# Attention with normalised q and k, planned by its own scheduler: first rows prepared separately, later second load, exact start times in the plan, last stores after the branch

## Chip, cores and metric

One core of one Trainium2 chip. The metric is the device time of one execution in microseconds (us). The kernel before ran three times: 594.15, 594.32 and 594.42 us, median 594.32 us. A measurement of this kernel can tell about 0.2% (1.2 us) from no change.

## The reference

There are 32 heads of 2048 rows and 20 columns, in bf16. For each head

```
qn = q / (sqrt(sum(q*q)) + 1e-6)          # each row by its own length
kn = k / (sqrt(sum(k*k)) + 1e-6)
logits = (qn @ kn.T) * t[head]
out = softmax(logits) @ v
```

Every head has 2048 x 2048 logits, 134 million in all, and each needs an exponential. The matrix products are thin (20 columns), so the exponentials are the bulk of the work.

## The kernel before

**Units of work.** Heads are taken in eight groups of four (`hg`), and the queries of a group in four blocks of 512 columns, so there are 32 blocks of four heads. A *unit* is one head's 128 keys against one block's 512 queries; a block has 64 units (4 heads x 16 key rows `r`), the kernel 2048. The four heads lie on four 32-partition strips, so their matmuls run beside each other on TensorE (PE).

**Two ways to the exponential.** Way A: two units are multiplied into psA (L793), and ScalarE (ACT) takes one `exp` over 128x1024 (L995, a *wave*). Way D: one unit is multiplied into a bank of psD (also L793), VectorE (DVE) turns it into int16 bits of an f16 by a scale and an offset (L361, called `P1`), GpSimd (POOL) makes two shifted copies by an integer addition (L374), and the sum of four products with v (L815, "PV") approximates the exponential. D units are taken four at a time (one key row of all four heads, a *quad*). At the end of a block DVE transposes the result (L386, the drain), divides (L400, L401), and a DMA stores it.

**Preparation.** Per group, q and k are squared and summed on DVE, their inverse lengths found, rows scaled into qpad and kpad, and these are transposed into qT and kT by DMA (L446) or, for the first key rows of group 0, by PE matmuls with an identity (L624, L658) and copies out of psum (L636, L639, L664). In group 0 rows 0 to 3 of q and k go first and together: `prep_ops(0, 0, 4, 0, 2)` gives one square, one sum, one root on ACT, then 1e-6, the reciprocal, k's scaling, t into q's factor, q's scaling. Rows 4 to 15 of k and then of q follow with priority 1.5.

**The order of the work** is made at build time: `make_plan` simulates the five engines in steps of `DT` = 0.005 us with costs per operation (`dve`: 0.069 us plus a rate; `ACT0`: 0.0633 us plus columns), picks for each engine the best ready operation by priority (P1 has 1, a lower number goes first), and writes down each engine's order. On the chip the engines follow those orders and wait on semaphores only. An operation of the plan begins at the step at which the loop sees it. `ORDER` is a string with one letter for each ten waves; a letter picks a set of rules from `CHOICES`. `D_FROM` = 0.12 is the share of a group's 256 units that must be issued before way D begins. `HEAT0` = 18 matmuls on zeros run on PE at the start, and `step_heat` puts 128-column ones into later PE gaps. A group's loads are asked for by `plan_group` on SyncE's (SP) queue, for group 1 as soon as `LOAD1` = 0 allows it.

**Branch on t.** There are two plans, one with way D and one without it. The first instructions are common; then each engine loads a flag (L1432) and branches (L1433). The last two stores, one on SP's queue and one on ACT's, are inside the branch; behind it only SP waits for them (L1439), and then all engines meet (L173).

Of the kernel before, what the change touches and what calls it, by code (L numbers as in the profile page):

```python
# [33 lines left out]
ORDER = "01i6e8h7238em08g57h5hi2i0gi1j2i0lgea8aa50a567i6538abh965h237050"  # L34

PARTS = ((0, 4), (4, 16))
NH = 4
# [7 lines left out]
D_FROM = 0.12  # L45
# [14 lines left out]
DT = 0.005  # L60
# [4 lines left out]
HEAT0 = 18  # L65
# [6 lines left out]
ACT0 = .0633  # L72
LOAD0 = 2.75
TRL = 2.25
TRK = 1.2
# [15 lines left out]
LOAD1 = 0  # L91
# [65 lines left out]
def bass_standalone__qk_norm__prompt_kernel(  # L157
# [15 lines left out]
    with ExitStack() as es:  # L173
# [45 lines left out]
        out_sems = {}  # L219

# [27 lines left out]
        def prep_ops(hg, r0, r1, a0=0, a1=2, pool=False):  # L248
# [106 lines left out]
            return ops  # L355

# [112 lines left out]
        def make_plan(share):  # L469
# [88 lines left out]
            for ap_, x, key in zs:  # L558
                want_dve(Op("DVE", "z", lambda e, ap_=ap_, x=x: e.memset(ap_, x), ["idn"] * (key[0] == "idb"), [key], 0.07, 0.3), 0)
            n0 = [("num", a) for a in range(8)]  # L560
            for b in (1, 2, 3):
                want_dve(Op("DVE", "z", lambda e, b=b: e.tensor_single_scalar(n4[:, :, b:b + 1], n4[:, :, 0:1], float(b), ALU.add),
                            n0, [("num", -b)], 0.08, 0.4), 0)
            nums = n0 + [("num", -b) for b in (1, 2, 3)]
            want_dve(Op("DVE", "z", lambda e: e.transpose(numT, num), nums, ["numT"], 0.15, 0.4), 0)
            want_dve(Op("DVE", "z", lambda e: e.tensor_tensor(numE, num, numT, ALU.is_equal), nums + ["numT"], ["numE"], 0.15, 0.4), 1.6)
            i4, e4 = idn[:, :].rearrange("p (a b) -> p a b", b=32), bass.AP(accT, numE.offset, [numE.ap[0], [0, 4], [1, 32]])
            want_dve(Op("DVE", "z", lambda e: e.tensor_tensor(i4, i4, e4, ALU.mult), ["idn", "numE"] + [("idb", a) for a in range(4)], ["idn", ("accT", 0)], 0.25, 0.4), 1.6)
# [6 lines left out]
            def t_load():  # L575
                src = bass.AP(t.tensor, 0, [[0, 128], [1, H]])
                want_sp(dma("ldt", lambda e: e.dma_start(tb16[:, :], src), [], ["tb"], 0.1, 3.2))
                want_dve(dve("flag", H, R1, lambda e: e.tensor_reduce(tmx[:, :], tb16[:, :], AXIS_X, ALU.max, apply_absolute_value=True), ["tb"], ["flag"]), 1.4)
                want_dve(Op("DVE", "z", lambda e: e.memset(tb2[:, :, :, :], 1.0), [], ["tb1"], 0.1, 0.2), 1.45)
                want_dve(dve("z", H, R1, lambda e: e.tensor_copy(tb2[:, :, 0, :], tb16[:, :].rearrange("p (g h) -> p g h", h=NH)), ["tb1", "tb"], ["tb2"]), 1.45)  # L580
# [13 lines left out]
            for o in prep_ops(0, 0, 4, 0, 2):  # L594
                if o.name == "nrm":
                    o.eng = "ACT"
                    act_ops.append(P.link(o))
                    a = Op("ACT", "tab", lambda e: e.activation(act_scr[:, 16:32], act_scr[:, 16:32], ACT.Exp),
                           ["scr"], ["scr1"], 1.5, 1.6)
# [22 lines left out]
            psQ = psD[:, QW:2 * QW]  # L622
            for w_, pad, T, bank, key in (("k", kpad, kT, psD, ("psD", 0)), ("q", qpad, qT, psO, ("psD", OB(0)))):
                mms = [lambda e, r=r, w_=w_, pad=pad, bank=bank: e.matmul((bank if w_ == "k" or r < 2 else psQ)[:, r * 128:(r + 1) * 128],  # L624
                                                                   pad[0][:, r, :, :].rearrange("p h d -> p (h d)"), idn[:, :])
                       for r in range(4)]
                op = Op("PE", "T" + w_, None, [(w_ + "pad", 0, r) for r in range(4)] + [(w_ + "z", 0), "idn"],
                        [key] + [("psD", 1)] * (w_ == "q"))
                op.info = mms
                pe_pre.append(P.link(op))  # L630

            kk, qq = [("kT", 0, r) for r in range(4)], [("qT", 0, r) for r in range(4)]
# [16 lines left out]
            pe_mid = []  # L649
            gate = ("qT", 0, 1)  # L650
            for r0, r1, a0, a1 in ((4, 16, 1, 2), (4, 16, 0, 1)):
                for o in prep_ops(0, r0, r1, a0, a1):
                    if o.name == "sq":
                        o.reads.append(gate)
                    want_dve(o, 1.5)
                if a0 == 1:

                    mms = [lambda e, r=r: e.matmul(psD[:, (r - 4) * 128:(r - 3) * 128],  # L658
                                                   kpad[0][:, r, :, :].rearrange("p h d -> p (h d)"), idn[:, :]) for r in range(4, 8)]
                    op = Op("PE", "Tk", None, [("kpad", 0, r) for r in range(4, 8)] + [("kz", 0), "idn"], [("psD", 0)])  # L660
                    op.info = mms
                    pe_mid.append(P.link(op))
# [4 lines left out]
                    gate = ("kT", 0, 7)  # L667
# [192 lines left out]
            def pv_round(c):  # L860
# [85 lines left out]
            def step_pe0():  # L946
                nonlocal a_sb, d_sb, issued_a, issued_d
                if pe_pre:
                    if all(d.done is not None and d.done + SEML <= now for d in pe_pre[0].deps):
                        pe_put(pe_pre.pop(0), "tp", range(NH))  # L950
                        return True
                    return False
                if pe_mid and all(d.done is not None and d.done + SEML <= now for d in pe_mid[0].deps):
                    pe_put(pe_mid.pop(0), "tp", range(NH))
# [179 lines left out]
            def step_act():  # L1134
# [7 lines left out]
                finish(a, now, a.cost, a.lat)  # L1142
                free_["ACT"] = now + a.cost
# [55 lines left out]
            def step_dve():  # L1199
# [6 lines left out]
                else:  # L1206
                    dve_todo.remove(best)
                    if o.name == "P1" and o.info[0] + 1 < DBANKS and (sum(x[2].name == "P1" for x in dve_todo) >= S.JOINB or next_wave() < JOINT) and sum(not kept(b_) for b_ in range(DBANKS)) >= S.JOINK:
                        nxt = next((x for x in dve_todo if x[2].name == "P1" and x[2].info == (o.info[0] + 1, o.info[1] + 1)), None)
                        if nxt is not None and ready_at(nxt[2]) is not None and ready_at(nxt[2]) <= now + S.JOIN:  # L1210
# [5 lines left out]
                            st = max(now, ready_at(o))  # L1216
# [4 lines left out]
                finish(o, now, o.cost, o.lat)  # L1221
                free_["DVE"] = now + o.cost
# [186 lines left out]
        def issue(eng, e, plan, i0, i1):  # L1409
            P, waits = plan  # L1410
            outs = [o for o in P.order["SP"] + P.order["ACT"] if o.name == "out"]
            for o in P.order[e][i0:i1]:
                if e == "SP" and o.name == "out" and o.sem is ends[0]:
                    for x in outs:
                        if x.sem not in ends:
                            eng.wait_ge(x.sem, 16)
# [7 lines left out]
                elif o.sem is not None:  # L1424
                    o.emit(eng).then_inc(o.sem, 16)
# [3 lines left out]
        def run(eng, e):  # L1429
# [5 lines left out]
            with eng.Else():  # L1435
                issue(eng, e, plans[1], cut[e], None)
            if e == "SP":
# [50 lines left out]
```

## Time and profile before

| what | value |
|---|---|
| median of 3 runs | 594.32 us |
| the profiled execution's own time | 594.49 us |
| its span, first to last instruction | 592.7 us |
| busy: PE, DVE, ACT, POOL | 581.3, 574.6, 580.4, 500.9 us |
| exp on ACT | 628 instructions, 576.2 us |
| P1 on DVE | 768 instructions, 488.1 us |
| first exp begins, last exp ends | 9.47 us, 585.96 us |

The profiled execution is 1.79 us longer than its span: that part lies around the recorded instructions. Times inside the trace are counted from the span's start. ACT and DVE are both busy through nearly the whole span, and the two ways share the units between them, so the time is read as three pieces: the head before the first exp, the stretch of exps, and the tail behind the last one.

### The profile page before, as it was taken

To read this page: it belongs to the slowest core of one execution; us is meant where nothing else is said; L and a number is where in the kernel's file an instruction comes from. 1 tells how busy PE (TensorE), PEld (TensorE's weight loads), DVE (VectorE), ACT (ScalarE), POOL (GpSimd) and SP (SyncE) were. 2 spreads that over 40 slices of the span, in tenths; PEclk is the share of its full clock that TensorE was granted. 3 is DMA by queue.
4 is the path that set the end of the run, shared out by engine and by line. 5 is a ranking of instruction groups with operands and counts; after the bars stand their busy time and mean duration, and the time that the engine had idled before them with its cause. 6 is when DMAs were issued, how large, how long until landed. Compare 5 with 4: busy or idle time off the path is not lost.

```text
span 592.7 us, 16383 instructions
## 1 busy us (share of the span) xinstructions
PE 581.3 (98%) x6768; PEld 160.2 (27%) x6768; DVE 574.6 (97%) x1016; ACT 580.4 (98%) x636; POOL 500.9 (84%) x951
## 2 busy tenths in 40 slices
PE   8999999999999999999999999999999999999996
PEld 4432222322223222232223222222222232222221
DVE  7999999999999999999999999999999999999993
ACT  6999999999999999999999999999999999999995
POOL 2488899878988799887998889987999978999994
PEclk9999999999999999999999999999999999999999
DMA  8700405205051131504033005330406104010000
GB/s 116 108 2 14 104 2 45 47 8 110 3 59 32 31 86 13 79 1 101 19 22 71 1 19 100 24 69 10 92 2 76 32 2 72 2 25 4 7 11 11
DMA packets 132145, 24.20 MB, mean 41 GB/s; under 512 B 121312, under 2 KB 132064, under 8 KB 132064
## 3 DMA queue, kind: packets, MB, share of 16 engines
q1 hardware_dynamic: 131264, 22.96, 24.6%
q8 instruction: 55, 0.90, 0.6%
q14 instruction: 26, 0.21, 0.1%
q10 hardware_dynamic: 800, 0.12, 0.1%
HBM read 7.87 MB, written 2.62 MB: 18 GB/s over the span
## 4 chain that ended last, share of the span: by engine, by line
ACT 87%; PE 10%; DVE 2%; POOL 1%; issue 0%
ACT pA L995 87%; PE psD L815 4%; PE psA L793 3%; PE psA L616 1%; PE psD L612 1%; POOL dS L374 1%; DVE dI L361 0%; PE psD L793 0%; PE psD L749 0%; DVE ssum L294 0%; DVE accT L386 0%; DVE sqs L291 0%; DVE kpad L338 0%; PE psD L616 0%; DVE ost L401 0%
## 5 line engine op out<-in xcount | busy, mean ns | idle before, releaser
L995 ACT ACTIVATE pA<-psA 128x1024 f16<-128x1024 f32 (+1 forms) x628 | 576.2, 1201 | 0.5 <-PE psD L793 0.2
L374 POOL INT64_ADD dS<-dI x935 | 494.5, 545 | 71.3 <-DVE ost L401 14.3
L361 DVE TENSOR_SCALAR dI<-psD 128x512 int16<-128x512 f32 (+1 forms) x768 | 488.1, 695 | 4.3 <-PE psD L793 2.5
L793 PE MATMUL psA<-qT,kT 32*128 32x512 bf16 x1256 | 246.4, 384 | 3.7 <-ACT pA L995 1.0
L793 PE MATMUL psD<-qT,kT 32*128 32x512 bf16 x795 | 237.6, 383 | 0.1
L815 PE MATMUL psD<-dS,vaug 128*22 128x512 f16 x1584 | 201.2, 383 | 0.1
L815 PE MATMUL psD<-pA,vaug 128*22 128x512 f16 (+1 forms) x1256 | 181.1, 383 | 0.3 <-POOL dS L374 0.3
L815 PE MATMUL psD<-dI,vaug 128*22 128x512 f16 x792 | 133.9, 383 | 0.0
L815 PE MATMUL psD<-dI,vhalf 128*22 128x512 f16 x792 | 131.4, 383 | 0.0
L793 PEld LDWEIGHTS psA<-qT,kT 32*128 32x128 bf16 x1256 | 59.0, 90 | 241.1 <-ACT pA L995 235.5
L793 PEld LDWEIGHTS psD<-qT,kT 32*128 32x128 bf16 x795 | 57.3, 91 | 11.1 <-DVE dI L361 4.8
L815 PEld LDWEIGHTS psD<-dS,vaug 128*22 128x22 bf16 x1584 | 42.9, 89 | 58.2 <-issue 38.2
L815 PEld LDWEIGHTS psD<-pA,vaug 128*22 128x22 bf16 x1256 | 39.6, 89 | 49.6 <-issue 41.2
L815 PEld LDWEIGHTS psD<-dI,vhalf 128*22 128x22 bf16 x792 | 29.7, 89 | 27.4 <-issue 20.0
L815 PEld LDWEIGHTS psD<-dI,vaug 128*22 128x22 bf16 x792 | 30.3, 89 | 23.4 <-issue 16.7
L386 DVE STREAM_TRANSPOSE accT<-psD 128x512 f32<-128x512 f32 x32 | 22.6, 705 | 4.6 <-PE psD L815 4.6
L401 DVE TENSOR_TENSOR ost<-accT,rec 128x320 bf16<-128x320 f32 x32 | 17.0, 532 | 0.1
L264 DVE TENSOR_TENSOR sqs<-qk 128x1280 bf16<-128x1280 bf16 x14 | 11.7, 835 | 0.0
L749 PE MATMUL psD<-ind,sqT 128*128 128x128 bf16 x140 | 11.3, 220 | 0.0
L612 PE MATMUL psD<-zt 128*128 128x128 bf16 x123 | 10.3, 221 | 0.0
L749 PEld LDWEIGHTS psD<-ind,sqT 128*128 128x128 bf16 x140 | 7.9, 98 | 4.5 <-issue 3.6
L612 PEld LDWEIGHTS psD<-zt 128*128 128x128 bf16 x123 | 7.0, 98 | 4.9 <-issue 4.9
(59 smaller groups left out, 84.7 us busy)
## 6 DMA issues: line engine op xcount, KB each, us to landing
vaug<-in_v_dram SPq DMA_DIRECT2D x32, 80.0 KB, 4.3
qk<-in_k_dram SPq DMA_DIRECT2D x7, 320.0 KB, 4.0
out_dram<-ost SPq DMA_DIRECT2D x28, 80.0 KB, 1.9
qk<-in_q_dram SPq DMA_DIRECT2D x6, 320.0 KB, 4.3
qk<-in_q_dram SPq DMA_DIRECT2D x4, 80.0 KB, 3.0
out_dram<-ost SPq DMA_DIRECT2D x7, 40.0 KB, 2.1
qk<-in_k_dram SPq DMA_DIRECT2D x1, 240.0 KB, 3.7
qk<-in_q_dram SPq DMA_DIRECT2D x1, 240.0 KB, 4.3
```

Of the source, the lines that this page charges most:

```text
L264: ops.append(dve("sq", w_, R2, lambda e, o=sq, x=x3: e.tensor_tensor(o, x, x, ALU.mult), [("qk", b, a, i) for i in parts] + [("qkx", b, i) ...
L361: lambda e: e.tensor_scalar(dst, psD[:, pb * QW:(pb + n) * QW], 1024.0 * LOG2E, 15360.0 - 1024.0 * LOG2K + SHIFTS[0], ALU.mult, ALU.add),
L374: lambda e: e.int64_add(o.bitcast(U64), x.bitcast(U64), add), rd, wr)
L386: return dve("drain", QW, R1, lambda e: e.transpose(accT[:, 16 * b:16 * b + 16, :].rearrange("p b d -> p (b d)"), psO_(sb)), [("psD", OB(s ...
L401: dve("omul", 320 * n, R1, lambda e: e.tensor_tensor(dst, num, rcb, ALU.mult), at + ar, [("ost", hg % 2, g) for g in range(g0, g1)]),
L612: return lambda e: e.matmul(bank, zt[:, 0:128], zt[:, 0:n], start=False, stop=False, skip_group_check=True)
L616: o.info = [lambda e: e.matmul(psO[:, :], zt[:, 0:128], zt[:, :])] + [(lambda e, i=i: e.matmul(psA[:, (i % 3) * QW:(i % 3 + 1) * QW], zt[: ...
L749: mms = [lambda e, g=g, j=j: e.matmul(dst, sqT[:, (5 * g + j) * 128:(5 * g + j + 1) * 128], ind[:, j, 96 - 32 * g:224 - 32 * g], start=g + ...
L793: return lambda e: e.matmul(dst, lhsT, rhs, tile_position=(32 * hh, 0))
L815: return lambda e: e.matmul(dst, lhsT, rhs, start=first, stop=last, skip_group_check=True, tile_position=(0, 32 * hh))
L995: a = Op("ACT", "exp", lambda e, s=src, d=dst: e.activation(d, s, ACT.Exp), [("psA", slot)], [("pA", pslot, i) for i in range(WAVES[slot]) ...
```

## The change

1. `first_ops` replaces `prep_ops(0, 0, 4, 0, 2)`: q and k have a square, a sum, a root, a 1e-6 and a reciprocal each, on 16 values per partition where it was 32. Order: squares of q and k, sums, roots, then q's chain to its scaling, then k's, k's rows 0, 1 apart from rows 2, 3. The load of the exp table on ACT follows the second root. The identity's last two steps have priority 0 (were 1.6).
2. On PE: `HEAT0` 18 to 11; then 3 small zero matmuls, q's transposes, 3 more, k's rows 0, 1, 6 more; k's rows 2, 3 later into a bank of their own. The copies out of psum: q's halves on DVE and ACT, k's rows 0, 1 on ACT, rows 2, 3 on DVE. No heating from `step_heat` before the first wave.
3. `D_FROM` 0.12 to 0.07; `LOAD1` 0 to 0.12: group 1's loads wait for that share of group 0. q's rows 4 to 15 no longer wait for `kT` row 7, and `kT` rows 8 to 15 and q's rows go by DMA as before.
4. The plan's costs: DVE 0.069 to 0.065, ACT0 0.0633 to 0.0634, `TRK` (extra time for group 0's k transpose) 1.2 to 2.0, some start-up operations; begin times are exact (`exact`) instead of rounded up to 0.005 us; a new `ORDER`.
5. The last `omul` (L401) signals a semaphore of its own, `fin_sem`. Both last stores move behind the branch and wait for it; SP's wait for the earlier stores moves there too.

```diff
-ORDER = "01i6e8h7238em08g57h5hi2i0gi1j2i0lgea8aa50a567i6538abh965h237050"
+ORDER = "47k7jh8jae711d87ll61hbhdg66k1j0aacegffef2fbk7ckemlia13g1h9am7k3"
-D_FROM = 0.12
+D_FROM = 0.07
-HEAT0 = 18
+HEAT0 = 11
+WARM = (3, 3, 6)
+CPQ = ("DVE", "ACT")
-ACT0 = .0633
+ACT0 = .0634
-TRK = 1.2
+TRK = 2.0
-LOAD1 = 0
+LOAD1 = .12
...
-            o = Op("DVE", name, emit, reads, writes, cost=0.069 + c + ncols_fix,
+            o = Op("DVE", name, emit, reads, writes, cost=0.065 + c + ncols_fix,
...
+        def first_ops():
...
+            return sqf + redf + nrmf + [epsf[0]] + invf[0:2] + [scf[0], epsf[1], invf[2]] + scf[1:]
...
+            def exact(eng, op, other=0.0):
+                st = max(free_[eng], ready_at(op) or 0.0, other)
+                return st if now - DT < st <= now else now
...
-            for o in prep_ops(0, 0, 4, 0, 2):
+            nrms = 0
+            for o in first_ops():
                 if o.name == "nrm":
-                    o.eng = "ACT"
                     act_ops.append(P.link(o))
+                    nrms += 1
+                    if nrms < 2:
+                        continue
...
+            pe_pre.extend([warm(WARM[0]), turn("q", 0, 4, [psO, psO, psQ, psQ], [("psD", OB(0)), ("psD", 1)]), warm(WARM[1]),
+                           turn("k", 0, 2, [psD] * 2, [("psD", 0)]), warm(WARM[2])])
+            pe_mid = [turn("k", 2, 4, [psK] * 2, [("psD", 2)])]
...
-            copy("ACT", kT, psD, 0, 128, [("psD", 0)], kk[:1])
-            copy("DVE", qT, psO, 0, 256, [("psD", OB(0))], qq[:2])
-            copy("ACT", qT, psQ, 256, 512, [("psD", 1)], qq[2:])
-            copy("ACT", kT, psD, 128, 512, [("psD", 0)], kk[1:])
+            copy(CPQ[0], qT, psO, 0, 256, [("psD", OB(0))], qq[:2])
+            copy(CPQ[1], qT, psQ, 256, 512, [("psD", 1)], qq[2:])
+            copy("ACT", kT, psD, 0, 256, [("psD", 0)], kk[:2])
+            copy("DVE", kT, psK, 256, 512, [("psD", 2)], kk[2:])
...
-                        o.reads.append(gate)
+                        o.reads.append(("qT", 0, 1))
...
+                            if o.name == "omul" and cur == NSB - 1:
+                                o.sem, o.val = fin_sem, 1
...
-                if in_use() >= S.HEAT or cur == NSB or not cur_free():
+                if not waves or in_use() >= S.HEAT or cur == NSB or not cur_free():
...
+                if o.name == "out" and o.sem in ends:
+                    assert o is P.order[e][-1] and [d.sem for d in o.deps] == [fin_sem]
+                    continue
...
             with eng.Else():
                 issue(eng, e, plans[1], cut[e], None)
+            if e == "SP":
+                for x in plans[0][0].order["SP"]:
+                    if x.name == "out" and x.sem not in ends:
+                        eng.wait_ge(x.sem, 16)
+            for o in plans[0][0].order[e][-1:]:
+                if o.name == "out":
+                    eng.wait_ge(fin_sem, 1)
+                    o.emit(eng).then_inc(o.sem, 16)
```

More of the change, by code (lines that the diff above doesn't have):

```diff
@@ L558, in make_plan @@
             for ap_, x, key in zs:
-                want_dve(Op("DVE", "z", lambda e, ap_=ap_, x=x: e.memset(ap_, x), ["idn"] * (key[0] == "idb"), [key], 0.07, 0.3), 0)
+                want_dve(Op("DVE", "z", lambda e, ap_=ap_, x=x: e.memset(ap_, x), ["idn"] * (key[0] == "idb"), [key], 0.07, 0.2), 0)
             n0 = [("num", a) for a in range(8)]
@@ L562, in make_plan @@
                 want_dve(Op("DVE", "z", lambda e, b=b: e.tensor_single_scalar(n4[:, :, b:b + 1], n4[:, :, 0:1], float(b), ALU.add),
[L563 removed]
+                            n0, [("num", -b)], 0.15, 0.2), 0)
             nums = n0 + [("num", -b) for b in (1, 2, 3)]
[L565 to L566 removed]
+            want_dve(Op("DVE", "z", lambda e: e.transpose(numT, num), nums, ["numT"], 0.15, 0.22), 0)
+            want_dve(Op("DVE", "z", lambda e: e.tensor_tensor(numE, num, numT, ALU.is_equal), nums + ["numT"], ["numE"], 0.15, 0.2), 0)
             i4, e4 = idn[:, :].rearrange("p (a b) -> p a b", b=32), bass.AP(accT, numE.offset, [numE.ap[0], [0, 4], [1, 32]])
[L568 removed]
+            want_dve(Op("DVE", "z", lambda e: e.tensor_tensor(i4, i4, e4, ALU.mult), ["idn", "numE"] + [("idb", a) for a in range(4)], ["idn", ("accT", 0)], 0.2, 0.28), 0)
             o = P.link(Op("ACT", "tab", lambda e: e.activation(act_scr[:, 0:16], act_scr[:, 0:16], ACT.Sqrt),
@@ L620, in make_plan, with turn, warm @@
             used_w = [(0.0, 0.0)]
[L622 to L630, printed above, removed]
+            psQ, psK = psD[:, QW:2 * QW], psD[:, 2 * QW:3 * QW]
+            def turn(w_, r0, r1, banks, keys):
+                pad = kpad if w_ == "k" else qpad
+                op = Op("PE", "T" + w_, None, [(w_ + "pad", 0, r) for r in range(r0, r1)] + [(w_ + "z", 0), "idn"], keys, cost=TS / 4 * (r1 - r0))
+                op.info = [lambda e, r=r, bank=bank: e.matmul(bank[:, (r % 4) * 128:(r % 4 + 1) * 128],
+                                                              pad[0][:, r, :, :].rearrange("p h d -> p (h d)"), idn[:, :])
+                           for r, bank in zip(range(r0, r1), banks)]
+                return P.link(op)
+            def warm(n):
+                op = Op("PE", "heat", None, ["zt"], [("psA", 1)], cost=TS / 4 * n)
+                op.info = [lambda e: e.matmul(psA[:, 3 * QW:3 * QW + 128], zt[:, 0:128], zt[:, 0:128])] * n
+                return P.link(op)
+            pe_pre.extend([warm(WARM[0]), turn("q", 0, 4, [psO, psO, psQ, psQ], [("psD", OB(0)), ("psD", 1)]), warm(WARM[1]),
+                           turn("k", 0, 2, [psD] * 2, [("psD", 0)]), warm(WARM[2])])
+            pe_mid = [turn("k", 2, 4, [psK] * 2, [("psD", 2)])]
             kk, qq = [("kT", 0, r) for r in range(4)], [("qT", 0, r) for r in range(4)]
@@ L653, in make_plan @@
                     if o.name == "sq":
-                        o.reads.append(gate)
+                        o.reads.append(("qT", 0, 1))
                     want_dve(o, 1.5)
                 if a0 == 1:
[L658 to L662, printed above, removed]
+                    pe_mid.append(turn("k", 4, 8, [psD] * 4, [("psD", 0)]))
                     keys = [("kT", 0, r) for r in range(4, 8)]
@@ L949, in step_pe0 @@
                     if all(d.done is not None and d.done + SEML <= now for d in pe_pre[0].deps):
-                        pe_put(pe_pre.pop(0), "tp", range(NH))
+                        pe_put(pe_pre[0], "tp", range(NH), pe_pre.pop(0).cost)
                         return True
@@ L953, in step_pe0 @@
                 if pe_mid and all(d.done is not None and d.done + SEML <= now for d in pe_mid[0].deps):
-                    pe_put(pe_mid.pop(0), "tp", range(NH))
+                    pe_put(pe_mid[0], "tp", range(NH), pe_mid.pop(0).cost)
                     return True
@@ L1141, in step_act @@
                     return False
-                finish(a, now, a.cost, a.lat)
-                free_["ACT"] = now + a.cost
+                st = exact("ACT", a)
+                finish(a, st, a.cost, a.lat)
+                free_["ACT"] = st + a.cost
                 n_act += 1
@@ L1215, in step_dve @@
                             o.deps += [d for d in nxt[2].deps if d not in o.deps]
-                            st = max(now, ready_at(o))
+                            st = max(exact("DVE", o), ready_at(o))
                             finish(o, st, o.cost, o.lat)
@@ L1220, in step_dve @@
                             return True
-                finish(o, now, o.cost, o.lat)
-                free_["DVE"] = now + o.cost
+                st = exact("DVE", o, lock[0] if o.port else 0.0)
+                finish(o, st, o.cost, o.lat)
+                free_["DVE"] = st + o.cost
                 return True
```

38 lines of the change are left out of this document (28 added, 10 removed).

## Prediction

> **What bounds the kernel now.** I read the page first, for the busy shares and the costliest lines.
>
> ```profile
> span 592.7 us, 16383 instructions
> ...
> PE 581.3 (98%) x6768; PEld 160.2 (27%) x6768; DVE 574.6 (97%) x1016; ACT 580.4 (98%) x636; POOL 500.9 (84%) x951
> ...
> L995 ACT ACTIVATE pA<-psA 128x1024 f16<-128x1024 f32 (+1 forms) x628 | 576.2, 1201 | 0.5 <-PE psD L793 0.2
> ```
>
> ACT does 628 exps and stands idle 0.5 us in front of them. One exp takes 576.2/628 = 0.9175 us of ACT, a unit 0.459 us. (The 1201 ns is one exp's whole duration; neighbours overlap.) PE's 98% says little, since the plan fills its gaps with heating. So the time is the moment of the first exp, plus 628 x 0.9175, plus what follows the last exp. Next the table by stages, to see who has room.
>
> ```profile
> 0.00:9.47 9.47, 7.66 (x32) 3.12 (x33) 5.94 (x34) 4.22 (x9) 3.51 (x10) 1.00 0.75 95
> 9.47:23.30 13.83, 13.53 (x154) 7.30 (x153) 11.54 (x29) 13.83 (x16) 2.86 (x6) 1.00 0.92 117
> ```
>
> ```profile
> 100.00:580.00 480.00, 477.31 (x5613) 126.80 (x5613) 477.07 (x818) 480.00 (x524) 421.72 (x796) 1.00 0.23 39
> ```
>
> The columns are PE, PEld, DVE, ACT, POOL. From 100 to 580 us ACT has no idle time and DVE 480 - 477.07 = 2.93 us: way A and way D are balanced. From 9.47 to 23.30 us DVE has 13.83 - 11.54 = 2.29 us idle, POOL far more. The head has DVE and ACT half idle: a chain of dependent steps. Three terms follow: head, middle, tail.
>
> **Head.** The timeline from the first data to the first exp (start, duration):
>
> ```profile
> 1.65 6.38 PE L616 MATMUL psA<-zt 128*128 128x512 bf16 x17
> ...
> 3.68 0.49 DVE L291 TENSOR_TENSOR sqs<-qk 128x640 bf16<-128x640 bf16 x1 [0.62 <-DMA qk<-in_q_dram]
> ...
> 4.29 0.81 DVE L294 TENSOR_REDUCE ssum<-sqs 128x32 f32<-128x640 bf16 x1
> ...
> 5.14 0.23 ACT L309 ACTIVATE nr<-ssum 128x32 f32<-128x32 f32 x1 [2.29 <-DVE ssum L294]
> 5.39 1.28 ACT L598 ACT_TABLE_LOAD   x1
> 5.40 0.18 DVE L310 TENSOR_SCALAR rsa<-nr 128x32 f32<-128x32 f32 x1
> ...
> 5.62 0.35 DVE L322 RECIPROCAL rn<-rsa 128x32 f32<-128x32 f32 x1
> ...
> 6.00 0.49 DVE L338 TENSOR_TENSOR kpad<-qk,rn 128x320 bf16<-128x320 bf16 x1
> ...
> 6.41 0.17 DVE L344 TENSOR_TENSOR rn<-rn,tb 128x16 f32<-128x16 f32 x1
> ...
> 6.61 0.49 DVE L338 TENSOR_TENSOR qpad<-qk,rn 128x320 bf16<-128x320 bf16 x1
> ...
> 6.77 0.76 PEld L616 LDWEIGHTS psA<-zt 128*128 128x128 bf16 x4 [0.28 <-issue]
> ...
> 8.09 0.39 PE L624 MATMUL psD<-idn,qpad 128*128 128x128 bf16 x4
> ...
> 8.51 0.38 ACT L636 ACTIVATE qT<-psD 128x256 bf16<-128x256 f32 x1
> 8.51 0.42 DVE L639 CAST qT<-psD 128x256 bf16<-128x256 f32 x1 [1.41 <-PE psD L624]
> ...
> 9.04 0.40 PE L793 MATMUL psA<-qT,kT 32*128 32x512 bf16 x4 [0.56 <-DVE qT L639]
> ...
> 9.47 7.48 ACT L995 ACTIVATE pA<-psA 128x1024 bf16<-128x1024 f32 x8 [0.19 <-PE psA L793]
> ```
>
> qpad is ready at 6.61 + 0.49 = 7.10 us, but PE heats until 1.65 + 6.38 = 8.03 us, so q's transposes wait almost a microsecond. With 11 heats that cover goes: they come (6.77 - 1.65)/12 = 0.427 us apart while slow, so ten after the first end near 5.9 us, with three small ones at 6.2. Then q's own chain is late next. Pieces of half the width (their durations):
>
> ```profile
> L294 DVE TENSOR_REDUCE ssum<-sqs 128x16 f32<-128x320 bf16 x2 | 1.0, 486 | 0.1
> ...
> L291 DVE TENSOR_TENSOR sqs<-qk 128x320 bf16<-128x320 bf16 x2 | 0.6, 318 | 0.0
> ```
>
> Squares of q and k begin 3.68 and 3.92 (about 0.08 of each duration overlaps the next instruction), sums 4.16 and 4.56, q's done at 4.65, root on ACT 4.69 to 4.91. DVE is free of k's sum at 4.96: 1e-6 at 4.96, reciprocal at 5.18 (the 0.22 between rows L310 and L322), t at 5.48 (0.38 there, 0.08 less for half the values), q's scaling at 5.68 (0.20), done 6.17. Transposes 6.24 to 6.63. k follows on DVE: 1e-6 6.09, reciprocal 6.31, rows 0 and 1 at 6.61, done 6.94, transposes to 7.28. k's root on ACT ends 5.31, table load 1.28 and its use 0.22, so ACT is free at 6.82: q's half until 7.20, k's 256 columns 7.31 to 7.69. Then as before 0.11 to the first product and 0.43 more to the exp: 8.23. Two small DVE operations (flag, copy of t), 0.1 each, may now lie in this chain: I take 8.40. **Head: 9.47 - 8.40 = 1.07 us.** Bounds: 1.24 with nothing in between, and 0.3 if PE's clock is slow (below). Twelve extra small matmuls stand on PE in its waits; only the last six, 0.3 to 0.6 us ahead of the first product, could show, and ACT's copy of k covers them.
>
> **Tail.** The end of the timeline and the rows of the branch (L1433) and of the final meeting (L173; duration, start):
>
> ```profile
> 582.95 3.01 ACT L995 ACTIVATE pA<-psA 128x1024 f16<-128x1024 f32 x3
> 588.46 0.67 ACTq L458 DMA_DIRECT2D out_dram<-ost  x1
> ```
>
> ```profile
> 587.94 0.49 DVE L401 TENSOR_TENSOR ost<-accT,rec 128x320 bf16<-128x320 f32 x1
> ```
>
> ```profile
> L1433 DVEq COMPARE_BRANCH  x1: 51/51/51, 588.0 to 588.0; - x1
> ...
> L1433 ACTq COMPARE_BRANCH  x1: 47/47/47, 589.2 to 589.2; - x1
> ```
>
> ```profile
> L173 SPq DRAIN  x1: 13/13/13, 591.1 to 591.1; - x1
> L173 ACTq DRAIN  x1: 81/81/81, 592.4 to 592.4; - x1
> ```
>
> ACT leaves the branch at 589.2, after its store, and does its next instruction 3.2 us later. SP, which waits for both stores to land, is through at 591.1. So ACT's way out of the branch ends last, by 1.3 us. [...]
>
> After the change ACT has nothing in the branch behind its last exp. DVE's branch (588.0) comes just after its last instruction began (587.94), before that ended. So ACT's would come with its last exp's start, 582.95 + 2 x 0.9175 = 584.8, and be through at 588.0, before the store's data at 588.43. Only the store queues behind ACT's new wait; on SP the store and the final waits. The stores go out as now, SP ends last. **Tail: 592.4 - 591.1 = 1.3 us.** If ACT branched only after its exp (585.96), its store would go at 589.2 and the gain be 0.5: the lower bound.
>
> **Middle.** A unit moved from A to D frees 0.459 us of ACT and costs DVE one P1. The last run of them:
>
> ```profile
> 574.25 8.03 DVE L361 TENSOR_SCALAR dI<-psD 128x512 int16<-128x512 f32 x13
> ```
>
> That is 8.03/13 = 0.62, or 0.61 without the end of the last. DVE time d that comes free is shared: d/(0.61 + 0.459) units move, so 0.43 d is gained. Way D opens at 0.12 x 256 = 31 units; with 0.07 at 18. The first P1 now:
>
> ```profile
> 23.32 6.57 DVE L361 TENSOR_SCALAR dI<-psD 128x1024 int16<-128x1024 f32 x9 [1.10 <-PE psD L793]
> ```
>
> DVE waits 1.10 us for it. With 18 units it opens with the ninth wave, at 8.40 + 7 x 0.9175 = 14.8 us, while DVE still has preparation to do, so the gaps of that stretch can be filled: of its 2.29 us I take 1.9. **Middle: 0.43 x 1.9 = 0.8 us.** The new cost per DVE operation, 0.004 us less, makes the plan claim 0.004 x 1016 = 4.1 us that it left before; the trace has 2.93 us idle from 100 to 580. I count zero for that and for the new ORDER, whose letters no row prices: at best 0.43 x 2.93 = 1.3 us, at worst one quad (two exps, 1.84 us) lost. Exact begin times and the ACT0 step change the plan only, and count there too.
>
> Group 1's later loads free SP's queue for the transpose of k's rows 8 to 15, which stood behind three loads:
>
> ```profile
> 11.79 5.33 SPq L437 DMA_DIRECT2D vaug<-in_v_dram  x3
> 17.16 2.05 SPq L446 DMA_TRANSPOSE kT<-kpad  x1
> ```
>
> ```profile
> kT<-kpad SPq DMA_TRANSPOSE x1, 4.0
> qT<-qpad SPq DMA_TRANSPOSE x1, 4.4
> ```
>
> (last: us from issue to landing). Those rows land now at 17.16 + 4.0 = 21.2; with the copies 1.2 us earlier and the queue free, they go out near 13.1 and land near 17.1. Eighteen of rows 0 to 7's 32 units are issued at 14.8; 14 more at 1/0.459 + 1/0.61 = 3.82 per us last to 18.5. So the earlier D stands on the later load, with 1.4 us in hand. Without it ACT would wait about 2.7 us. The loads' own delay is covered by group 0's remaining 225 units, some 59 us.
>
> **Sum.** 594.49 - 1.07 - 1.3 - 0.8 = 591.3; the median lies 0.17 under the profiled execution: **591.2 us**, own range 590.2 to 592.4.
>
> **Rivals.**
> *q starved (slower).* P1 has priority 1, the preparation of q's rows 4 to 15 priority 1.5.
>
> ```profile
> 15.41 0.73 DVE L291 TENSOR_TENSOR sqs<-qk 128x640 bf16<-128x640 bf16 x2
> ...
> 19.66 0.66 DVE L338 TENSOR_TENSOR qpad<-qk,rn 128x960 bf16<-128x960 bf16 x1
> ```
>
> It takes 15.41 to 20.32, 4.9 us, and 4.4 to land. Block 0's 46 remaining units last until 14.8 + 46/3.82 = 26.8, so it must begin by 17.5. If P1s took every turn it would begin at 26.8: ACT idle 9.3, DVE 4.4, (9.3 x 2.18 + 4.4 x 1.64)/3.82 = 7.2 us, **598.4**. It eats the whole gain once the beginning slips past 17.5 + 3.1 x 3.82/2.18 = 22.9. For it: the nine P1s above leave DVE no gap. Against: the plan feeds a new D unit only when no P1 waits, and only two quads' worth of rows is there before 17.1.
>
> *Slow PE clock.* PE's heats come 0.427 us apart up to 6.77, then (0.76 - 0.10)/3 = 0.22: the clock opened 5.5 us after the first, though the PEclk column says 1.00. With heats to 6.2 only, it may stay slow. Transposes and product cost 0.4; PE is full in the stretch (13.53 of 13.83), so ACT loses half of what stays slow. Another 5.5 us after 6.77 is 12.3, (12.3 - 8.4)/2 + 0.4 = 2.35: **593.5**. [...]
>
> *More D.* All the idle of the body is used and a full quad moves: 0.43 x (1.9 + 2.93) = 2.1 in the middle, then also 0.17 in the head and some ORDER: **589.3**.
>
> [...]
>
> **Chances.** Forecast 0.58, more D 0.10, slow clock 0.10, no effect 0.10, q starved 0.12. A measurement here tells about 0.2%, 1.2 us, from no change: below 593.1 is faster, above 595.5 slower. Faster 0.58 + 0.10 + half the slow clock = 0.73; same 0.05 + 0.10 = 0.15; slower 0.12. The range 589.3 to 594.2 leaves out q starved and half of more D, 0.17.
>
> **What would show it.** First exp near 8.4 us, right after a copy of k and not after heats; ACT's branch near its last exp and SP's drain last, some 5.1 us after that exp; 624 to 628 exps without idle; first P1 near 15 us; qT's transpose issued before 22 us. Idle in front of L995 near 27 us means q starved; small matmuls 0.11 us apart after 8 us mean the clock. More than 630 exps would make the middle wrong.

## The result and the profile after

The changed kernel takes **598.19 us** (median of 6 runs, 597.82 to 599.45) beside 594.37 us (median of 6, 593.94 to 594.62) for the kernel before: a ratio of 1.0069 with a 95% interval of 1.0056 to 1.0082. It is 0.7% slower. The forecast was 591.2 us and faster, so both the sign and the range were wrong. The profiled execution took 597.82 us, its span is 596.1 us.

First the same lines of the page as were read of before: the span, the busy shares, and the exps on ACT.

```profile
span 596.1 us, 16347 instructions
...
PE 579.6 (97%) x6747; PEld 156.6 (26%) x6747; DVE 577.3 (97%) x1018; ACT 577.1 (97%) x632; POOL 505.3 (85%) x957
...
L1037 ACT ACTIVATE pA<-psA 128x1024 f16<-128x1024 f32 (+1 forms) x624 | 573.0, 1204 | 10.6 <-PE psA L833 8.2
```

There are 624 exps instead of 628, 3.2 us less of ACT. But ACT now stands idle 10.6 us in front of them, where it was 0.5 us. The table by stages shows where (columns: PE, PEld, DVE, ACT, POOL, each busy us and count, then the granted clock of PE, the busy share of the DMA engines and GB/s).

```profile
0.00:7.78 7.78, 5.84 (x37) 2.72 (x38) 6.23 (x39) 4.05 (x9) 3.52 (x10) 1.00 0.69 103
7.78:18.98 11.20, 9.82 (x106) 5.02 (x104) 10.54 (x32) 10.28 (x11) 2.66 (x5) 1.00 0.60 76
18.98:25.81 6.83, 1.61 (x12) 0.38 (x16) 1.22 (x3) 0.01 (x2) 2.90 (x8) 0.69 0.99 136
25.81:35.28 9.47, 9.47 (x68) 1.63 (x68) 7.14 (x12) 7.05 (x7) 6.42 (x11) 0.50 0.16 10
...
100.00:580.00 480.00, 476.96 (x5625) 126.19 (x5621) 477.62 (x808) 480.00 (x525) 423.33 (x794) 1.00 0.24 39
...
590.94:596.10 5.16, 0.72 (x16) 0.20 (x8) 1.46 (x3) 0.00 (x0) 0.18 (x1) 0.89 0.12 25
```

The body from 100 to 580 us is as before or a little better: ACT has no idle time, DVE 2.38 us (2.93 before). The loss is in two neighbouring rows near the start. From 18.98 to 25.81 us PE, DVE and ACT nearly stand still (1.61, 1.22 and 0.01 us busy). From 25.81 to 35.28 us PE is always busy, at a granted clock of 0.50, and ACT works only 7.05 of 9.47 us. ACT's timeline shows the same as waits (start, duration, idle time before it and who ended it):

```profile
7.78 3.77 ACT L1037 ACTIVATE pA<-psA 128x1024 bf16<-128x1024 f32 x4 [0.49 <-PE psA L833]
12.46 6.52 ACT L1037 ACTIVATE pA<-psA 128x1024 f16<-128x1024 f32 x7 [0.92 <-PE psA L833]
25.81 1.02 ACT L1037 ACTIVATE pA<-psA 128x1024 f16<-128x1024 f32 x1 [6.82 <-PE psA L833]
27.31 1.94 ACT L1037 ACTIVATE pA<-psA 128x1024 f16<-128x1024 f32 x2 [0.48 <-PE psD L833]
...
35.28 555.66 ACT L1037 ACTIVATE pA<-psA 128x1024 f16<-128x1024 f32 x606 [0.49 <-PE psD L833]
```

ACT waits for PE. To see what PE waited for, the timeline of all engines up to the standstill's end:

```profile
10.09 0.79 PE L651 MATMUL psD<-zt 128*128 128x128 bf16 x11
...
11.71 0.40 PE L855 MATMUL psD<-pA,vaug 128*22 128x512 bf16 x4 [0.83 <-DMA vaug<-in_v_dram]
...
16.09 3.68 DVE L393 TENSOR_SCALAR dI<-psD 128x512 int16<-128x512 f32 x6
...
16.81 0.38 POOL L571 MEMSET vaug<- 128x64 bf16 x1
...
22.91 4.67 POOL L406 INT64_ADD dS<-dI  x10 [5.72 <-issue]
...
24.20 0.60 PE L855 MATMUL psD<-dS,vaug 128*22 128x512 f16 x2 [5.46 <-POOL dS L406]
...
25.38 1.29 DVE L393 TENSOR_SCALAR dI<-psD 128x512 int16<-128x512 f32 x2 [5.61 <-PE psD L833]
```

Read it backwards from the last line. DVE waits 5.61 us for PE, PE waits 5.46 us for POOL, and POOL's first addition begins at 22.91 us after 5.72 us of "issue": nothing that the profile shows held it. Its data was there soon after DVE's first P1 had begun, at 16.09 us, and POOL was free from 17.19 us on, when its last zero fill ended. (The line at 11.71 is ACT's first wait, 0.92 us: PE's first PV waits for v's load.) What stands in those 5.72 us is found among the instructions of the addition's line in both kernels, after and before:

```profile
L406 POOLq MODIFY_POOL_CONFIG  x2: 6/6/6, 17.2 to 17.2; - x2
```

```profile
L374 POOL INT64_ADD dS<-dI x10: 388/388/815, 25.4 to 29.8; - x10
...
L374 POOLq MODIFY_POOL_CONFIG  x2: 11/11/11, 19.2 to 19.2; - x2
```

POOL reaches its first integer addition at 17.2 us (19.2 before), and the first one begins 5.7 us later (6.2 before). Before, the first P1 came only at 23.32 us, so nearly all of the same delay lay behind other work, and POOL's timeline of before put the idle time down to DVE:

```profile
25.35 7.38 POOL L374 INT64_ADD dS<-dI  x14 [6.93 <-DVE dI L361]
```

The first P1, 1.23 us long at most, was done by 24.55 us; the addition began 0.8 us later. What POOL does in the 5.72 us of the changed kernel isn't shown: between its two configurations, at 17.15 and 17.19 us, and the addition at 22.91 the trace has no row of POOL. The experiments test the delay, whatever POOL does in it.

### The profile page after: what moved, and what is told of

Read it like the earlier page. It is cut to its first block, busy times and chain, and to the rows that moved or that the text cites. A ratio compares the mean times of both kernels' runs of the same rounds, so it can differ in the third digit from the quotient of the medians.

```text
span 596.1 us, 16347 instructions
## 1 busy us (share of the span) xinstructions
PE 579.6 (97%) x6747; PEld 156.6 (26%) x6747; DVE 577.3 (97%) x1018; ACT 577.1 (97%) x632; POOL 505.3 (85%) x957
## 2 busy tenths in 40 slices
DMA packets 132145, 24.20 MB, mean 41 GB/s; under 512 B 121312, under 2 KB 132064, under 8 KB 132064
## 3 DMA queue, kind: packets, MB, share of 16 engines
q1 hardware_dynamic: 131264, 22.96, 24.4%
## 4 chain that ended last, share of the span: by engine, by line
ACT 90%; PE 6%; SPq 1%; DVE 1%; DMA 1%; issue 1%; POOL 0%
ACT pA L1037 90%; PE psD L855 3%; PE psA L833 2%; SPq L469 1%; DMA vaug<-in_v_dram 1%; DVE dI L393 1%; PE psD L833 0%; PE psD L651 0%; SPq L459 0%; POOL dS L406 0%; DVE accT L418 0%; DVE ost L433 0%; SPq L613 0%; DVE rec L432 0%; PE psD L666 0%
## 5 line engine op out<-in xcount | busy, mean ns | idle before, releaser
L1037 ACT ACTIVATE pA<-psA 128x1024 f16<-128x1024 f32 (+1 forms) x624 | 573.0, 1204 | 10.6 <-PE psA L833 8.2
L833 PE MATMUL psD<-qT,kT 32*128 32x512 bf16 x804 | 240.5, 387 | 0.2
L855 PE MATMUL psD<-dS,vaug 128*22 128x512 f16 x1600 | 203.5, 386 | 5.5 <-POOL dS L406 5.5
L855 PE MATMUL psD<-pA,vaug 128*22 128x512 f16 (+1 forms) x1248 | 174.8, 385 | 0.8 <-DMA vaug<-in_v_dram 0.8
L855 PE MATMUL psD<-dI,vhalf 128*22 128x512 f16 x800 | 129.7, 382 | 0.0
L833 PEld LDWEIGHTS psD<-qT,kT 32*128 32x128 bf16 x804 | 58.5, 91 | 10.2 <-DVE dI L393 4.2
L855 PEld LDWEIGHTS psD<-pA,vaug 128*22 128x22 bf16 x1248 | 37.4, 89 | 45.8 <-issue 39.6
L432 DVE RECIPROCAL rec<-accT 128x16 f32<-128x16 f32 x32 | 7.5, 235 | 0.1
L325 DVE RECIPROCAL rn<-rsa 128x128 f32<-128x128 f32 (+1 forms) x9 | 7.4, 827 | 0.0
```

Source lines behind the costliest of these rows:

```text
L325: add("inv", lambda e: e.reciprocal(rn_, ra), [K("ra")], RN[a0:a1], R1, n * 5 * R1)
L432: dve("rec", 16 * n, R1, lambda e: e.reciprocal(rc, aT[:, :, D]), at, ar, 16 * n * 5 * R1),
L833: return lambda e: e.matmul(dst, lhsT, rhs, tile_position=(32 * hh, 0))
L855: return lambda e: e.matmul(dst, lhsT, rhs, start=first, stop=last, skip_group_check=True, tile_position=(0, 32 * hh))
L1037: a = Op("ACT", "exp", lambda e, s=src, d=dst: e.activation(d, s, ACT.Exp), [("psA", slot)], [("pA", pslot, i) for i in range(WAVES[slot]) ...
```

## The experiments

The theory (**POOL**): way D opens too early for POOL's start-up; PE keeps to its order and stands at the first PV on POOL's result, and ACT and DVE stand behind PE; PE's clock closes in that pause and costs some more. The rivals: the later load of group 1 (**LOAD1**); the earlier D by itself (**D_FROM**); the new **ORDER**; the slower **clock** as a cause of its own. All ratios are against the kernel before, run on the same chip. It took 594.2 to 594.3 us on these chips, so the times can be set beside the changed kernel's too, to about 0.2 us.

### pool_early: the addition's start-up taken early

Both selects come together, and right behind them an addition into a scratch tile takes the start-up; group 1's zero fills, which stood between, go behind the twelfth real addition.

```diff
+        pscr = sbuf("pscr", [128, 16], I16)
...
+                pre = Op("POOL", "pre", lambda e: e.int64_add(pscr[:, :].bitcast(U64), ind[:, 0, 0:16].bitcast(U64), 0), [], [], .1, .1)
...
+                s2.start, pre.start = late[0].start - 2e-4, late[0].start - 1e-4
...
+                for i, o in enumerate(late):
+                    o.start = runs[11].start + 1e-4 * (i + 1)
```

> The changed kernel, all other engines' orders kept; on POOL the second mask operation and one extra integer addition on a scratch tile stand ahead, so that POOL's second configuration comes right after the masks, and group 1's zeros are moved behind the twelfth addition. [...] Load theory (group 1's loads, now at 17.5 to 25 us, hold up POOL's start): the first real addition still comes near 22.9 and the time stays near 598.

Measured: 593.04 us (10 runs, 590.79 to 598.85), ratio 0.9981 (0.9958 to 1.0004), 5.2 us under the changed kernel. POOL's timeline, then ACT's:

```profile
12.12 0.76 POOL L577 TENSOR_SCALAR_AFFINE_SELECT ind<-ind 128x160 bf16<-128x160 bf16 x2 [7.88 <-DVE rsi L319]
18.60 0.18 POOL L1381 INT64_ADD pscr<-ind  x1 [5.72 <-issue]
18.78 5.82 POOL L407 INT64_ADD dS<-dI  x12
```

```profile
21.03 1.02 ACT L1038 ACTIVATE pA<-psA 128x1024 f16<-128x1024 f32 x1 [1.82 <-PE psA L834]
22.29 1.94 ACT L1038 ACTIVATE pA<-psA 128x1024 f16<-128x1024 f32 x2 [0.23 <-PE psD L834]
```

The 5.72 us of "issue" have moved to the scratch addition, whole; the twelve real ones follow without a gap, 4.1 us earlier. This addition needs nothing of DVE, so a wait for data is excluded. Group 1's loads are excluded too: SP asks for them from 17.50 us on in the changed kernel, whose order SP keeps here, and the delay runs from 12.88 to 18.60. The standstill shrinks from 6.82 to 1.82 us. That is the largest part of the loss, and nothing of the way D's opening, the load or ORDER was touched. The runs spread over 8 us, and they go by the granted clock of the whole execution: 590.79 and 591.09 at 0.999, 592.25 to 592.73 between 0.993 and 0.997, 593.35 to 593.64 at 0.990 and 0.991, 598.85 at 0.983. So a second cost is left, which varies with PE's clock. The theory gave 588.5 to 590.5 us; that was missed for this reason, and because the first real addition came at 18.78 us and not before 18.

### load1_0: group 1's load as before

```diff
-LOAD1 = .12
+LOAD1 = 0
```

> The changed kernel with LOAD1 = 0, planned anew: group 1's loads come early as in the kernel before. Load theory: with those loads away from 17 to 25 us POOL's gap between configuration and first addition falls below 2 us, no standstill, about 590 us. [...]

Measured: 605.94 us (4 runs, 604.55 to 607.57), ratio 1.0208 (1.0186 to 1.0229). A standstill of 5.69 us is still there, behind the same delay on POOL (the timelines of ACT and POOL; then the body in the table by stages):

```profile
26.69 1.02 ACT L1037 ACTIVATE pA<-psA 128x1024 f16<-128x1024 f32 x1 [5.69 <-PE psA L833]
```

```profile
24.32 2.38 POOL L406 INT64_ADD dS<-dI  x4 [6.04 <-issue]
```

```profile
100.00:580.00 480.00, 476.82 (x5527) 127.74 (x5527) 465.45 (x777) 480.00 (x524) 418.47 (x820) 1.00 0.25 39
```

The later load is not the cause of the standstill. The surprise, and the reason why the time lies above the 595 to 599 us that the theory gave, is the body: DVE idles 480 - 465.45 = 14.55 us there instead of 2.38. With another LOAD1 the plan is made anew, and the letters of ORDER then meet other states.

### dfrom12: way D opened as before

```diff
-D_FROM = 0.07
+D_FROM = 0.12
```

> The changed kernel with D_FROM = 0.12, planned anew: way D opens at 31 units, near 7.8 + 14 x 0.9175 = 20.6 us, the first additions are wanted near 22. [...] Load theory: the loads lie at the same place, so several us of standstill remain, above 594 us.

Measured: 600.49 us (4 runs, 599.31 to 606.08), ratio 1.0138 (1.0097 to 1.0179). The 589 to 591.5 us that the theory gave were missed, and for the reason just seen. ACT's timeline, the exps on the page, and the body:

```profile
12.36 14.99 ACT L1037 ACTIVATE pA<-psA 128x1024 f16<-128x1024 f32 x16 [0.69 <-PE psA L833]
```

```profile
L1037 ACT ACTIVATE pA<-psA 128x1024 f16<-128x1024 f32 (+1 forms) x634 | 582.2, 1187 | 2.0 <-PE psA L833 1.2
```

```profile
100.00:580.00 480.00, 477.50 (x5524) 127.92 (x5521) 467.42 (x791) 480.00 (x525) 421.95 (x827) 1.00 0.24 38
```

In the head it does what the theory says: sixteen exps run on through the time of the standstill, and ACT idles 2.0 us in all. But DVE idles 12.58 us in the body and 634 exps are needed, 10 more than the changed kernel's, 582.2 - 573.0 = 9.2 us. So it can't price D_FROM alone: it shows that the standstill needs the early opening, and suggests that ORDER belongs to one plan.

### tail_only: part 5 alone on the kernel before

```diff
+                                o.sem, o.val = fin_sem, 1
...
+            for o in plans[0][0].order[e][-1:]:
+                if o.name == "out":
+                    eng.wait_ge(fin_sem, 1)
+                    o.emit(eng).then_inc(o.sem, 16)
```

> The kernel before with only the last two stores moved behind the branch (part 5 of the change); the plan and all orders are the same. My theory: ACT's way out of the branch, 3.2 us, lies under the last drain, SP ends last, 1.3 to 1.6 us less: 592.7 to 593.1 us. Rival: ACT's way out only moves ahead of its store, 0 to 0.5 us less: 593.8 to 594.4 us.

Measured: 592.50 us (8 runs, 592.35 to 593.04) beside 594.28, ratio 0.997 (0.996 to 0.9981): 1.8 us gained, a little more than the 1.3 to 1.6 expected. The rows of the branch:

```profile
L1434 ACTq COMPARE_BRANCH  x1: 43/43/43, 584.7 to 584.7; - x1
```

The prediction put ACT's branch at 584.8 us; it is at 584.7. In ACT's timeline the last exp runs from 584.84 to 586.04 us, so the branch didn't wait for its end. The tail's step holds, alone and measured.

### warm_wait: the pause kept, PE kept busy in it

One hundred small zero matmuls stand in PE's queue ahead of the PV that waits for POOL.

```diff
+            for o, n in zip(late, (100,)):
...
+                h.info = [heat_mm(psO_(0)[:, 0:HEATN], HEATN)] * n
+                on.insert(on.index(o), h)
```

> The changed kernel with 100 small zero matmuls on PE inside the 5.5 us in which it waits for POOL, so that PE is busy there; POOL as in the changed kernel. [...]

Measured: 594.85 us (10 runs, 594.49 to 600.25), ratio 1.002 (1.0002 to 1.0037), 3.3 us under the changed kernel; the theory gave 595.3 to 596.3. ACT's timeline and a row of the table by stages:

```profile
25.21 1.02 ACT L1037 ACTIVATE pA<-psA 128x1024 f16<-128x1024 f32 x1 [6.27 <-PE psA L833]
26.46 19.36 ACT L1037 ACTIVATE pA<-psA 128x1024 f16<-128x1024 f32 x21 [0.22 <-PE psD L833]
```

```profile
20.00:25.00 5.00, 5.00 (x85) 4.34 (x82) 0.01 (x1) 0.00 (x0) 2.04 (x5) 1.00 0.94 144
```

The wait for POOL stays, 6.27 us, and the clock is 1.00 in this row. The five waits of nearly half a microsecond that followed in the changed kernel, 2.36 us together, are down to one of 0.22. The standstill is 0.55 us shorter too, though POOL's first addition begins at 22.96 us as before (22.91). So the half clock was a consequence of the pause and cost about 3.3 us, and the pause itself the rest. In one of the ten runs, the one of 600.25 us, the clock was 0.987 all the same; no profile shows where.

### pool_heat: pool_early with small matmuls in both pauses left

```diff
+            for o, n in zip(late, (18, 6)):
```

> pool_early with 18 and 6 small zero matmuls on PE ahead of the first two products that wait for POOL (1.0 and 0.3 us of waiting there), all else the same. Clock theory (what is left in pool_early is PE's clock, which closes to half at 22.2 us after those gaps and opens again at 32.4, and in some executions doesn't close): the clock stays open in every execution, exps follow without the 0.23 to 0.49 us waits after 22 us, span near 589, 590.5 to 591.2 us with a spread under 1 us. Rival (the waits after 22 us come from POOL's late start itself): the waits stay and the median stays near 593.

Measured: 592.79 us (6 runs, 591.40 to 593.56), ratio 0.9966 (0.9954 to 0.9977), clocks of 0.996 to 1.000. The 590.5 to 591.2 us expected, with little spread, were missed. None of these six runs is as long as the one of 598.85 us among pool_early's ten, which proves little. The profile still has a pause, by ACT's timeline and PE's waits:

```profile
29.00 1.02 ACT L1038 ACTIVATE pA<-psA 128x1024 f16<-128x1024 f32 x1 [1.56 <-PE psD L834]
```

```profile
PE psD L856 <- POOL dS L407: 1.4, 1, 1.4
```

This one comes from where pool_early put the zero fills: POOL does them from 24.94 us on, and PE waits for the addition behind them.

### best: pool_early, with the selects and the first wave freed

The selects no longer wait for k's scaled rows, and one pair of products for way A goes ahead of the first PV, which waited for v's load.

```diff
+                    o.deps = [d for d in o.deps if d.name != "nmk"]
...
+                on[j].start = on[i].start - 1e-4
+                on.insert(i, on.pop(j))
```

> [...] Theory: first real addition near 17 us, no gap on PE that closes the clock, 589.6 to 590.6 us. [...]

Measured: 593.14 us (12 runs, 590.89 to 600.48), ratio 0.9995 (0.9968 to 1.0022). No gain over pool_early in the median. By clock: 590.89 to 590.99 in the three runs at 0.999 and 1.000, 592.23 and 592.48 at 0.997, 593.12 to 594.92 from 0.991 to 0.988, 598.72 and 599.44 at 0.983, 600.48 at 0.978. Its wait for v is away (in its profile ACT's first run is seven exps instead of four). Freeing the selects did little, by POOL's timeline:

```profile
17.96 0.18 POOL L1384 INT64_ADD pscr<-ind  x1 [6.03 <-issue]
```

The selects begin 0.95 us earlier, at 11.17, but the delay is 0.31 longer, and the first real addition comes at 18.14 us, not near 17 as expected. What is left goes with PE's clock in the longer runs; in the profiled run, at 0.999, it is waits of PE for POOL, 2.4 us in all.

### order_old: the changed kernel with the ORDER of before

> The changed kernel with the string ORDER of the kernel before, so planned anew. The two kernels planned anew so far left DVE 12.6 and 14.5 us idle between 100 and 580 us, against 2.4 in the changed kernel and 2.9 in the kernel before. If ORDER fits only the plan that it was chosen for: DVE idle there 8 us or more and 601 to 606 us. If ORDER is worth little: DVE idle 2 to 4 us and 597 to 600 us.

Measured: 605.71 us (2 runs, 605.05 and 606.36), ratio 1.0191 (1.0173 to 1.0208). The exps on the page, and the body:

```profile
L1037 ACT ACTIVATE pA<-psA 128x1024 f16<-128x1024 f32 (+1 forms) x628 | 576.8, 1191 | 10.9 <-PE psD L833 7.7
```

```profile
100.00:580.00 480.00, 476.08 (x5566) 126.76 (x5558) 472.32 (x810) 480.00 (x525) 424.44 (x826) 1.00 0.25 39
```

With the old letters on the new costs and openings DVE idles 7.68 us in the body, and 628 exps are needed as before, 4 more than with the new ORDER. ACT still waits 10.9 us in all. The new ORDER is therefore not what made the change slower; on this plan it needs four exps fewer than the old one. Letters chosen anew for load1_0 or dfrom12 were not tried, so the misfit of letters and plan is the likely cause of their idle DVE, not a shown one.

### zeros_late and steady: what was left

zeros_late is best with the zero fills behind the 28th and the 37th addition. steady adds to it the 18 heats of before at the start (the plan still counts 11) and 12 small matmuls ahead of the first PV that waits for POOL.

```diff
-                    o.start = runs[11].start + 1e-4 * (i + 1)
+                    o.start = runs[36 if i > 1 else 27].start + 1e-4 * (i + 1)
```

```diff
-... for i in range(HEAT0 - 1)]
+... for i in range(HEAT0 + 6)]
...
+            for o, n in zip(late, (12,)):
```

> best with group 1's zeros on POOL not behind the 12th addition, where PE waited 1.4 us for POOL near 26 us, but behind the 28th and 37th, where POOL waits anyway; heating as in the changed kernel. If POOL's lateness alone makes what is left: the wait near 26 us goes, 590.0 to 590.8 us with little spread. If PE's clock also misses its opening in the head (best lay between 590.9 and 600.5, with mean clocks from 1.000 down to 0.978): the fastest executions gain about 1 us, but others stay at 592 to 600.

> zeros_late with 18 heats on PE at the start as in the kernel before (the plan still counts 11) and 12 small zero matmuls ahead of the first product that waits for POOL. Clock theory: mean clock 0.998 or more in every execution, spread under 1 us; the heats may hold the first exp up to 8.3 to 9.3 us: 590.3 to 592.0 us, faster than both kernels. Rival (the spread has another cause): 591 to 600 as in best.

Measured: zeros_late 590.15 us (6 runs, 589.58 to 593.67), ratio 0.994 (0.992 to 0.9961); steady 590.56 us (5 runs, 589.93 to 590.96), ratio 0.9941 (0.9928 to 0.9954). Both beat the kernel before by 0.6%. Two of zeros_late's runs, the profiled one among them, had a clock of 0.991 and took 593.5 and 593.7; all five of steady had 1.000. By the median steady is no faster than zeros_late; its runs lie closer together, within 1.03 us. The profiled run of zeros_late in steps of 1 us:

```profile
19.00:20.00 1.00, 0.10 (x4) 0.13 (x4) 1.00 (x2) 0.16 (x1) 1.00 (x4) 1.00 0.81 122
...
21.00:22.00 1.00, 0.85 (x12) 0.28 (x15) 0.93 (x2) 0.89 (x1) 1.00 (x4) 0.91 1.14 328
22.00:23.00 1.00, 1.00 (x11) 0.16 (x10) 0.72 (x2) 0.76 (x1) 1.00 (x2) 0.50 1.31 98
...
31.00:32.00 1.00, 1.00 (x11) 0.21 (x7) 0.26 (x1) 0.52 (x2) 0.40 (x1) 0.50 0.00 0
32.00:33.00 1.00, 1.00 (x16) 0.22 (x12) 0.87 (x2) 0.95 (x2) 0.47 (x1) 0.97 0.00 0
```

After a wait of PE of about a microsecond (from 19 to 20 us it is busy 0.10 us) the clock is at half for ten. In steady it isn't, though ACT's wait remains (its timeline):

```profile
8.35 6.52 ACT L1038 ACTIVATE pA<-psA 128x1024 bf16<-128x1024 f32 x7 [0.48 <-PE psA L834]
15.55 3.89 ACT L1038 ACTIVATE pA<-psA 128x1024 f16<-128x1024 f32 x4 [0.68 <-PE psA L834]
20.84 24.94 ACT L1038 ACTIVATE pA<-psA 128x1024 f16<-128x1024 f32 x27 [1.40 <-PE psA L834]
```

One wait of 1.40 us is what is left of POOL's start-up. The first exp comes at 8.35 us, 0.44 later than zeros_late's 7.91: that is the price of the heats, and the gain would be that no run pays for a closed clock.

## Why the prediction was wrong

Made against the profiled execution of before, the terms are these. Idle time of ACT is counted behind the first exp.

| term | predicted, us | measured, us |
|---|---|---|
| head: first exp at 7.78 instead of 9.47 | -1.07 | -1.69 |
| way D takes more units: exps 573.0 instead of 576.2 | -0.8 | -3.2 |
| ACT idle: 10.6 - 0.49 instead of 0.5 - 0.19 | 0 | +9.8 |
| tail: 5.16 behind the last exp instead of 6.74 | -1.3 | -1.58 |
| sum | -3.2 | +3.3 |

594.49 + 3.3 is the 597.82 us measured. Three terms have the right sign, and together they are twice as large as forecast. The fourth was not in the sum.

**The step that failed** is the one on the middle: "With 18 units it opens with the ninth wave, at 8.40 + 7 x 0.9175 = 14.8 us, while DVE still has preparation to do, so the gaps of that stretch can be filled". It asked who feeds the first P1 (PE's products, k's rows) and took P1 as the end of the step. It is the middle of a chain: DVE's P1, POOL's addition, PE's PV. The first addition could not begin before 17.2 + 5.7 = 22.9 us. The trace of before had this row: POOL's configuration at 19.2 us and its first addition at 25.4, though it named DVE for the idle time between. The prediction took POOL's idle time in this stretch as room ("POOL far more"). What hid the 5.7 us was the old opening of way D, and the text should have asked what that opening covered. pool_early shows this cause (5.2 us back by taking the start-up, and with it POOL's order around it, earlier), and warm_wait divides the cost: about 3.3 us of it are PE's half clock after the pause.

**Head.** The mechanism was right, and the term was mis-sized by 0.62. q's chain came as forecast. k's was earlier:

```profile
5.64 0.44 DVE L384 TENSOR_TENSOR qpad<-qk,rn 128x320 bf16<-128x320 bf16 x1
...
6.91 0.38 ACT L683 ACTIVATE kT<-psD 128x256 bf16<-128x256 f32 x1
...
7.34 0.40 PE L833 MATMUL psA<-qT,kT 32*128 32x512 bf16 x4
```

q's scaling begins at 5.64 (5.68 forecast), ACT's copy of k at 6.91 (7.31). DVE fits k's 1e-6 and reciprocal into q's chain, at 5.27 and 5.48 us in the timeline, which the working put behind it (6.09 and 6.31), and the added 0.17 us for small operations was not needed. What an earlier first exp then meets, v's load, which had not moved, the working didn't ask: 0.92 us of the idle time.

**Tail.** The mechanism was right, and its 1.3 us a little small: tail_only gains 1.8 us by itself. In the changed kernel SP's drain is last, as said:

```profile
L175 ACTq DRAIN  x1: 582/582/582, 594.0 to 594.0; - x1
...
L175 SPq DRAIN  x1: 13/13/13, 595.9 to 595.9; - x1
```

It comes 595.9 - 590.94 = 4.96 us behind the last exp (5.1 forecast).

**Middle.** ORDER was counted at zero, with 1.84 us as the worst case. The runs say otherwise in both directions: four exps, 3.7 us, between the new and the old letters on the new plan (order_old has 628), and 7.7 to 14.6 us of idle DVE in the body of the three kernels that were planned anew with one thing changed. The prediction took the gain from DVE's idle time in the head alone.

**The rivals.** q was not starved: its transpose is issued at 16.02 us, before the 22 that the prediction set as the bound. That this rival's price, 598.4 us, lies next to the 598.19 measured is chance. The slow clock in the head did not occur in the profiled execution, where the eleven small matmuls at 10.09 us (the timeline above) come (0.79 - 0.23)/10 = 0.056 us apart, and not 0.11. A slow clock came later, for a reason that the rival did not have: a pause of PE. That half of this rival's chance lay on the faster side was the author's estimate, which no run shows. The later load did no harm that a run shows. The first P1 came at 16.09 us, a microsecond after its forecast. No effect, with 0.10 among the chances, is excluded as well: the first exp came 1.69 us sooner, and tail_only gained 1.8 us by itself.

**Open.** Why a pause of some one to six microseconds is followed by about 6.8 us (load1_0), 10.2 us (pool_early, zeros_late) or 13.7 us (the changed kernel) at half clock, and why in some executions only, isn't settled. In best's profiled run PE was busy for 3.53 of 5.00 us between 25 and 30 us, with a wait of 1.5 us for POOL as its longest, and the clock stayed at 1.00. zeros_late against steady shows only that with more heat the clock stayed open in five runs of five, where it was four of six. Were four in six the rule, five of five would come by chance about once in eight times, so that the heats did it is likely and not shown; which of steady's two additions would do it wasn't tried.

## What to carry to other kernels

Before an engine's first use is moved forward, look in the trace at how long each engine down the chain took for the first of its kind, and what covered it: idle time between a configuration and the first operation behind it (5.7 us on POOL) was a start-up here, even where the profile named another engine for it, and a scratch operation took it early. Where an in-order engine serves two ways, one late partner of the one way stops both: PE's 5.46 us wait for POOL in way D stopped way A's exps for 6.82 us. A schedule tuned by letters is part of the plan that it was tuned on: change one constant alone, and what you measure can be mostly the misfit.

## What the runs showed of the hardware

- The first integer addition on POOL begins 5.72 us (after, pool_early), 5.98 (zeros_late), 6.04 (load1_0) or 6.11 us (steady) after POOL is free, also right behind selects, which POOL runs too. Zero fills between later additions cost no second start-up: in pool_early they begin at 24.54, and the next additions at 26.02 us.
- In the changed kernel PE stood from 18.74 to 24.20 us. Its clock fell near 21.5 us and was at 0.50 until near 35.2, about 13.7 us by the table in steps of 1 us, eleven of them with PE at work again. In pool_early, after about a microsecond of pause, it was at half for about 10.2 us. That PE is at work again doesn't open it at once: from 25.81 to 35.28 us PE is busy, as the profile counts it, for 9.47 of 9.47 us at 0.50.
- ACT's sequencer took its branch before the instruction ahead of it had ended: the branch came at 584.7 us in tail_only, and the last exp ended at 586.04.
